# The head of a one-core SSM and FFN kernel: where the mean of the first two tiles is taken off, and how these tiles are loaded

## The chip, the core and the metric

The kernel runs on one NeuronCore of a Trainium2 chip. The metric is the device time of one execution in microseconds (us); the median of three runs is 178.27, from 178.15 to 178.41. The core has five engines with instruction streams of their own: TensorE (PE in the profile, its weight loads PEld), VectorE (DVE), ScalarE (ACT), GpSimd (POOL) and SyncE (SP), which here only issues transfers. Transfers (DMAs) are issued from the queues of SyncE, ScalarE and GpSimd and run beside the engines. SBUF is the on-chip memory, PSUM the memory that TensorE writes its results to, in eight banks.

## What is computed

The reference normalises x (2048 tokens of 512 features) over the features, feeds the result to a diagonal state-space layer A and to a gated feed-forward layer B, and adds both to x:

```
xn = (x - mean) / sqrt(var + 1e-5)
A:  Bu = xn @ B_bar.T;  h[t] = Lam_bar * h[t-1] + Bu[t];  y = 2 * Re(h @ C.T) + xn * Dskip
B:  (silu(xn @ w_gate) * (xn @ w_up)) @ w_down        # w_gate, w_up: 512 x 1376
out = x + A(xn) + B(xn)
```

Everything comes and goes in bfloat16. State and features are 512, so each is four blocks of 128.

## The kernel before

The 2048 tokens are 16 tiles of 128 rows, in four chunks of 512 tokens. TensorE multiplies along the partition axis, so the normalised tokens are wanted transposed, features on the partitions. For chunks 1 to 3 a transposing DMA does this. Chunk 0 can't wait for it. Its first three tiles go another way: they are transposed by TensorE, by a matmul against the identity matrix, and only their mean is taken off (`xcT`); the factor 1 / sqrt(var + eps) of a token (`rstd`) is applied later, as a per-row scale, when the product of tokens and weights leaves PSUM (`sw_gate`, `sw_up`).

The order of the work on every engine is the order in which the program writes it down; no scheduler moves it. Each engine runs its own list in that order and waits where an operand isn't ready.

The start of the program (lines 119 to 136) issues the loads. SyncE loads tile 0 of x, then four rows of the up weights (`wu01`, 256 KB each; a row is 128 of the 512 features), two rows of the gate weights (`wg01`), tile 2, a third gate row, tile 3, the fourth gate row, and more. ScalarE loads tile 1. A memset by VectorE (line 124) of two elements of tile 1 is written ahead of that load, so that it waits for it. From the third gate or x load of SyncE on, an issue waits for the landing of an earlier transfer, because the completion semaphores are used in turn.

The head proper begins at line 692. TensorE runs nine warm-up matmuls on constants (`dummy`, four of 512 columns and five of 128), into a bank that is not needed yet. VectorE makes `minus_mean`, the identity times -1/512, and sums each of the first two tiles over its features (`sum_dve`, line 221). Then, for tile i = 0 and 1 and feature block k:

- `raw_mm(i)` (line 233) transposes the four blocks of raw tile i into PSUM, one matmul of 128 columns each (line 230).
- `cT_mean(i, ...)` (line 237) adds the negative mean to one block or two, by a matmul of the broadcast sum with `minus_mean` that accumulates on the transposed block.
- `raw_copy(i, k)` (line 241) copies the block out of PSUM to `xcT` (a part of the tile CF in the profile), even blocks on ScalarE, odd ones on VectorE (line 245).

`row_mm` (line 712) then multiplies both tiles by one weight row at a time: for k = 0 to 3 four matmuls of 128x512 (two tiles, two groups of 512 columns) with the up weights, and after them the same with the gate weights. In the profile they are line 487. They use all eight PSUM banks. While the up rows run, VectorE takes the statistics of both tiles (line 182), and ScalarE takes the up products out with their scale (line 507). Tiles 2 and 3, the state-space scans on VectorE and the rest of the feed-forward layer follow; TensorE then works through all chunks.

Of the kernel before, what the change touches and what calls it, by code (L numbers as in the profile page):

```python
# [12 lines left out]
ALU = mybir.AluOpType  # L13
# [10 lines left out]
def kernel(  # L24
# [17 lines left out]
    nc = tc.nc  # L42
# [7 lines left out]
    NCH = L // CW  # L50
    TPC = CW // 128
    KD = D // 128
# [21 lines left out]
    def bank(shape=(128, CW), dtype=F32):  # L74
        return psum.tile(list(shape), dtype, name="ps")
# [4 lines left out]
    x_v = A_x[0].rearrange("(n p) d -> p n d", p=128)  # L80
# [5 lines left out]
    xall = const.tile([128, NT, D], BF16, name="xall")  # L86
    xnT = const.tile([128, NCH, KD, CW], BF16, name="xnT")
# [31 lines left out]
    HK = KD // 2  # L119
    ident = const.tile([128, 128], BF16, name="ident")  # L120
    make_identity(nc, ident[:])
    minus_mean = const.tile([128, 128], BF16, name="minus_mean")
    nc.sync.dma_start(out=xall[:, 0, :], in_=x_v[:, 0, :])
    nc.vector.memset(xall[:, 1, 0:2], 0.0)
    nc.scalar.dma_start(out=xall[:, 1, :], in_=x_v[:, 1, :])
    nc.scalar.preload_act_table_set("silu_and_others")
    for k in range(KD):
        load_row(nc.sync, wu01, wu_v, k)
# [49 lines left out]
    def by_k(ap):  # L178
        return ap.rearrange("p (k d) -> p k d", d=128)
# [30 lines left out]
    xcT, xc = CF[:, 0], CF[:, 1]  # L210
# [5 lines left out]
    sums = const.tile([128, 2], BF16, name="sums")  # L216
# [4 lines left out]
    def sum_dve(i, dst):  # L221
        nc.vector.scalar_tensor_tensor(out=xnT[:, NCH - 1, i, 0:HW], in0=xall[:, i, 0:HW], scalar=1.0,
                                       in1=xall[:, i, HW:D], op0=ALU.mult, op1=ALU.add, accum_out=dst)

    pair = [[[bank() for _ in range(2)] for _ in range(2)] for _ in range(2)]
    warm = pair[0][0][1]
    raw = [pair[0][1] + pair[1][0], pair[1][1] * 2]

    def cT_mm(ps, src, k, first, stop):
        nc.tensor.matmul(ps[:, k * 128:(k + 1) * 128], lhsT=src[:, k * 128:(k + 1) * 128], rhs=ident[:], start=first,  # L230
                         stop=stop)

    def raw_mm(i):
        for k in range(KD):
            cT_mm(raw[i][k], xall[:, i, :], k, all(p is not raw[i][k] for p in raw[i][:k]), False)

    def cT_mean(i, *ks):
        nc.tensor.matmul(by_k(raw[i][ks[0]][:])[:, ks[0]:ks[-1] + 1:HK], lhsT=sums[:, i:i + 1].to_broadcast([128, 128]),  # L238
                         rhs=minus_mean[:, None, :].to_broadcast([128, len(ks), 128]), start=False, stop=True)

    def raw_copy(i, k):
        cT_copy(V.tensor_copy if k % 2 else nc.scalar.copy, raw[i][k], i, k, k + 1)

    def cT_copy(copy, ps, i, k0=0, k1=KD):
        copy(out=xcT[:, k0:k1, i * 128:(i + 1) * 128], in_=by_k(ps[:, k0 * 128:k1 * 128]))
# [21 lines left out]
    V = nc.vector  # L267
# [398 lines left out]
    def dummy(ps, n, cols):  # L666
        for _ in range(n):
            nc.tensor.matmul(ps[:, 0:cols], lhsT=one.to_broadcast([128, 128]), rhs=one.to_broadcast([128, cols]),
                             start=True, stop=True)
# [20 lines left out]

    G, U = wg_g, wu_g
    dummy(warm, 4, CW)
    dummy(warm, 5, 128)
    nc.vector.tensor_scalar(out=minus_mean[:], in0=ident[:], scalar1=-1.0 / D, scalar2=None, op0=ALU.mult)
    for i in range(2):
        sum_dve(i, sums[:, i:i + 1])
    raw_mm(0)
    for k in range(HK):
        cT_mean(0, k)
        raw_copy(0, k)  # L700
    raw_mm(1)
    for k in range(HK, KD):
        cT_mean(0, k)
    for k in range(HK):
        cT_mean(1, k, k + HK)
        raw_copy(1, k)
    for k in range(HK, KD):
        raw_copy(0, k)
    for k in range(HK, KD):
        raw_copy(1, k)  # L710

    def row_mm(which, k):
        for i in range(2):
# [191 lines left out]
```

## Time and profile before

| | us |
|---|---|
| median of the runs | 178.27 (178.15 to 178.41) |
| span of the profiled execution | 175.8 |
| TensorE busy in the span | 171.4 (97%) |
| VectorE busy in the span | 156.9 (89%) |
| ScalarE busy in the span | 102.0 (58%) |
| first weight matmul (line 487) | starts at 4.98 |

The span runs from the first to the last instruction of the profiled execution. No time of its own outside the span is given for that execution; against the median of the runs 2.5 us lie around the span. In rows of a timeline the first number is the start in us from the span's beginning, the second the duration, then engine, line, operation, output and input, and how many instructions stand together; in brackets, how long the engine was idle before and what ended that. SPq and ACTq are issues of transfers. In rows of the transfers, the last number is the time from issue to landing in us. In grouped rows, the numbers behind the bar are the busy time in us, the mean of one in ns and the idle time before them. In rows by stretches of time, each engine has its busy time and a count, then come the granted TensorE clock, the busy share of the DMA engines and GB/s.

### The profile page before, as it was taken

How to read it: one execution, taken by the hardware profiler on the slowest of the kernel's cores; microseconds unless marked ns; L12 is line 12 of the kernel's file. 1: busy time of each engine (PE TensorE's matmuls, PEld its weight loads, DVE VectorE, ACT ScalarE, POOL GpSimd, SP SyncE). 2: the span in 40 equal slices, each digit the busy share in tenths (PEclk: the TensorE clock that was granted, in tenths of full speed). 3: DMA queues.
4: the chain of work that ended last, by engine and by line, in shares of the span. 5: the costliest groups of instructions: out<-in, count | busy, mean ns of one | idle time of the engine just before them, and what ended most of it. 6: DMA issues, size and time to landing. Idle time of an engine off the chain costs nothing.

```text
span 175.8 us, 2365 instructions
## 1 busy us (share of the span) xinstructions
PE 171.4 (97%) x847; PEld 82.6 (47%) x863; DVE 156.9 (89%) x259; ACT 102.0 (58%) x188; POOL 28.1 (16%) x39
## 2 busy tenths in 40 slices
PE   8999999999999999999999999999999999999993
PEld 4544446464444444446444444446444444444542
DVE  3776999999999999999999999999999998699542
ACT  3379498793997685236598660024666653990100
POOL 5244110032000000044300000025000000522500
PEclk9999999999999999999999999999999999999999
DMA  5998929999999300047016000007200000696921
GB/s 184 344 350 83 245 48 205 285 191 300 161 218 306 112 4 0 0 38 82 2 34 119 0 0 0 0 0 87 36 15 17 0 4 0 87 175 96 117 66 60
DMA packets 34043, 17.88 MB, mean 102 GB/s; under 512 B 24896, under 2 KB 32928, under 8 KB 33984
## 3 DMA queue, kind: packets, MB, share of 16 engines
q1 hardware_dynamic: 30288, 14.22, 34.1%
q0 software_dynamic: 3456, 3.28, 14.4%
q10 hardware_dynamic: 288, 0.23, 0.4%
q8 instruction: 7, 0.11, 0.3%
q14 instruction: 4, 0.03, 0.1%
HBM read 8.03 MB, written 5.24 MB: 75 GB/s over the span
## 4 chain that ended last, share of the span: by engine, by line
PE 96%; DMA 1%; issue 1%; DVE 0%
PE ps L455 29%; PE ps L598 22%; PE ps L611 16%; PE ps L380 16%; PE ps L487 8%; PE ps L541 3%; PE ps L771 2%; DMA xall<-in_A_x_dram 1%; PE ps L230 1%; PE ps L238 0%; DVE xall L614 0%; PE ps L271 0%
## 5 line engine op out<-in xcount | busy, mean ns | idle before, releaser
L598 PE MATMUL ps<-wd_sb,guT 128*128 128x512 bf16 (+4 forms) x184 | 38.7, 366 | 0.2
L422 DVE TENSOR_TENSOR_SCAN g<-r_t,car,u 128x512 bf16<-128x512 f32 x24 | 29.1, 1264 | 0.0
L611 PE MATMUL ps<-CF,wt 128*128 128x512 bf16 (+2 forms) x134 | 28.4, 366 | 0.1
L380 PE MATMUL ps<-xnT,BT 128*128 128x512 bf16 x125 | 28.1, 379 | 0.2
L598 PEld LDWEIGHTS <-guT 128*128 128x128 bf16 (+1 forms) x187 | 17.9, 98 | 20.5
L455 PE MATMUL ps<-xnT,wu 128*128 128x512 bf16 x95 | 24.6, 379 | 0.2
L455 PE MATMUL ps<-xnT,wg 128*128 128x512 bf16 x91 | 23.9, 379 | 0.1
L618 POOL DMA_DIRECT2D out_dram<-res x12 | 10.5, 1043 | 77.3 <-ACT res L617 72.1
L469 ACT ACTIVATE guT<-ps 128x512 bf16<-128x512 f32 x30 | 18.3, 609 | 4.8 <-PE ps L455 4.5
L470 ACT CAST u<-ps 128x512 bf16<-128x512 f32 x30 | 17.9, 596 | 4.6 <-PE ps L455 4.5
L382 ACT CAST u<-ps 128x512 bf16<-128x512 f32 x32 | 17.5, 597 | 4.8 <-PE ps L380 3.3
L611 PEld LDWEIGHTS <-wt 128*128 128x128 bf16 x136 | 13.0, 98 | 14.7
L380 PEld LDWEIGHTS <-BT 128*128 128x128 bf16 x128 | 12.5, 98 | 14.8
L617 ACT CAST res<-ps 128x512 bf16<-128x512 f32 x12 | 6.8, 583 | 21.0 <-PE ps L611 21.0
L572 ACT ACTIVATE xr<-xall,nb,rstd 128x512 bf16<-128x512 bf16 x16 | 11.8, 805 | 9.1 <-DVE xall L580 4.9
L455 PEld LDWEIGHTS <-wu 128*128 128x128 bf16 x96 | 9.4, 98 | 11.3
L455 PEld LDWEIGHTS <-wg 128*128 128x128 bf16 x96 | 9.3, 98 | 10.6
L192 POOL TENSOR_TENSOR rstd<-ve,neg_half 128x1 f32<-128x1 f32 (+1 forms) x7 | 7.6, 1079 | 29.4 <-DVE ve L191 29.0
L455 PE MATMUL ps<-xnT,w_end 128*128 128x512 bf16 x48 | 10.9, 379 | 0.0
L182 DVE BATCH_NORM_STATS2 stats<-xall 128x6 f32<-128x512 bf16 x16 | 10.8, 675 | 0.0
L474 DVE TENSOR_TENSOR guT<-guT,u 128x1024 bf16<-128x1024 bf16 x15 | 10.0, 675 | 0.0
L390 DVE TENSOR_TENSOR pm<-g,c 128x2048 bf16<-128x2048 bf16 x8 | 9.8, 1220 | 0.1
(120 smaller groups left out, 207.8 us busy)
## 6 DMA issues: line engine op xcount, KB each, us to landing
out_dram<-in_A_x_dram SPq DMA_DIRECT2D x3, 512.0 KB, 5.3
out_dram<-res POOLq DMA_DIRECT2D x12, 128.0 KB, 3.1
out_dram<-xall POOLq DMA_DIRECT2D x3, 512.0 KB, 6.0
wd_sb<-in_B_w_down_dram SPq DMA_DIRECT2D x1, 1280.0 KB, 8.2
wu<-in_B_w_up_dram SPq DMA_DIRECT2D x4, 256.0 KB, 3.8
wg<-in_B_w_gate_dram SPq DMA_DIRECT2D x4, 256.0 KB, 4.8
xall<-in_A_x_dram SPq DMA_DIRECT2D x1, 1024.0 KB, 7.0
xall<-in_A_x_dram SPq DMA_DIRECT2D x1, 512.0 KB, 6.1
```

What stands on the lines that cost most here:

```text
L182: nc.vector.bn_stats(out=stats[:, n, 0, :], in_=xall[:, n, :])
L380: nc.tensor.matmul(ps[:] if c else by_k(ps[:]), lhsT=BT[:, part, k, q * 128:(q + 1) * 128], rhs=xnT[:, c, k, :] if c else xnT0[:, k], star ...
L382: nc.scalar.copy(out=u_tiles[c][:, part, q, :], in_=ps[:])
L422: V.tensor_tensor_scan(out=g()[:, part, q, :], data0=r_t[:, q:q + 1].to_broadcast([128, CW]), data1=u_tiles[c][:, part, q, :], initial=ini ...
L455: nc.tensor.matmul(ps[:fs, lo:hi], lhsT=wslice(groups, fi, k), rhs=xnT[:, c, k, lo:hi], start=(k == 0), stop=(k == KD - 1))
L469: nc.scalar.activation(out=guT[:fs, fi, :], in_=psg[:fs], func=ACT.Silu)
L470: nc.scalar.copy(out=u_pair[c][:fs, fi % 2, :], in_=psu[:fs])
L487: nc.tensor.matmul(ps[:, 0:(b - a) * 128], lhsT=tokens(i, k), rhs=groups[gi][:, k, 0:(b - a) * 128], start=(k == 0), stop=(k == KD - 1))
L572: nc.scalar.activation(out=box["xr"][:], in_=xall[:, n, :], func=ACT.Identity, scale=rstd[:, n:n + 1], bias=nb[:, n:n + 1])
L598: nc.tensor.matmul(o[:], lhsT=gu_tiles[c][:fsz[fi], fi, i * 128:(i + 1) * 128], rhs=wd_sb[:fsz[fi], fi, lo:hi], start=(fi == 0), stop=False)
L611: nc.tensor.matmul(o[:], lhsT=w_tiles[c][:, part, q, i * 128:(i + 1) * 128], rhs=CF[:, part, q, lo:hi], start=False, stop=(part == 1 and q ...
L618: nc.gpsimd.dma_start(out=out_v[:, n, lo:hi], in_=res[:, lo:hi], accum_op=ALU.add)
```

## The change

Tiles 0 and 1 are each loaded in two pieces, rows 0 to 87 on SyncE's queue and rows 88 to 127 on ScalarE's; the memset is gone. The warm-up has three matmuls of 128 columns instead of five. The mean is no longer accumulated on the transposed blocks: `mean_mm` makes it once for a tile, 128 columns into a bank of its own (`low`). `raw_copy` takes two raw blocks at a time out of PSUM on ScalarE into SBUF (`xrT`, a part of `xnT` that is written much later), and `centered` on VectorE adds the negative mean from PSUM while writing `xcT`, first block by block for blocks 0 and 1 of both tiles, then blocks 2 and 3 together.

```diff
-    nc.sync.dma_start(out=xall[:, 0, :], in_=x_v[:, 0, :])
-    nc.vector.memset(xall[:, 1, 0:2], 0.0)
-    nc.scalar.dma_start(out=xall[:, 1, :], in_=x_v[:, 1, :])
+    XS = 88
+    for i in range(2):
+        nc.sync.dma_start(out=xall[0:XS, i, :], in_=x_v[0:XS, i, :])
+        nc.scalar.dma_start(out=xall[XS:128, i, :], in_=x_v[XS:128, i, :])
...
-    raw = [pair[0][1] + pair[1][0], pair[1][1] * 2]
+    raw, low = (pair[0][1], pair[1][0]), pair[1][1]
+    xrT = xnT[:, NCH - 2]
...
     def raw_mm(i):
         for k in range(KD):
-            cT_mm(raw[i][k], xall[:, i, :], k, all(p is not raw[i][k] for p in raw[i][:k]), False)
-
-    def cT_mean(i, *ks):
-        nc.tensor.matmul(by_k(raw[i][ks[0]][:])[:, ks[0]:ks[-1] + 1:HK], lhsT=sums[:, i:i + 1].to_broadcast([128, 128]),
-                         rhs=minus_mean[:, None, :].to_broadcast([128, len(ks), 128]), start=False, stop=True)
-
-    def raw_copy(i, k):
-        cT_copy(V.tensor_copy if k % 2 else nc.scalar.copy, raw[i][k], i, k, k + 1)
+            cT_mm(raw[i][k // HK], xall[:, i, :], k, k % HK == 0, k % HK == HK - 1)
+
+    def raw_copy(i, h):
+        k0, k1 = h * HK, (h + 1) * HK
+        nc.scalar.copy(out=xrT[:, k0:k1, i * 128:(i + 1) * 128], in_=by_k(raw[i][h][:, k0 * 128:k1 * 128]))
+
+    def mean_mm(i):
+        nc.tensor.matmul(low[i][:, 0:128], lhsT=sums[:, i:i + 1].to_broadcast([128, 128]), rhs=minus_mean[:],
+                         start=True, stop=True)
+
+    def centered(i, k0, k1):
+        at = slice(i * 128, (i + 1) * 128)
+        V.tensor_tensor(out=xcT[:, k0:k1, at], in0=xrT[:, k0:k1, at],
+                        in1=low[i][:, None, 0:128].to_broadcast([128, k1 - k0, 128]), op=ALU.add)
...
-    dummy(warm, 5, 128)
+    dummy(warm, 3, 128)
...
-    raw_mm(0)
-    for k in range(HK):
-        cT_mean(0, k)
-        raw_copy(0, k)
-    raw_mm(1)
-    for k in range(HK, KD):
-        cT_mean(0, k)
-    for k in range(HK):
-        cT_mean(1, k, k + HK)
-        raw_copy(1, k)
-    for k in range(HK, KD):
-        raw_copy(0, k)
-    for k in range(HK, KD):
-        raw_copy(1, k)
+    for i in range(2):
+        raw_mm(i)
+        mean_mm(i)
+        for h in range(2):
+            raw_copy(i, h)
+    for i in range(2):
+        for k in range(HK):
+            centered(i, k, k + 1)
+    for i in range(2):
+        centered(i, HK, KD)
```

## The prediction

> **What bounds the kernel now.** I read the page's engine shares first, then the chain that ended last, then the waits of TensorE, and only then the first ten microseconds as a timeline.
>
> ```profile
> span 175.8 us, 2365 instructions
> ...
> PE 171.4 (97%) x847; PEld 82.6 (47%) x863; DVE 156.9 (89%) x259; ACT 102.0 (58%) x188; POOL 28.1 (16%) x39
> ...
> PE 96%; DMA 1%; issue 1%; DVE 0%
> ```
>
> TensorE carries 96% of the chain; the only other visible piece, DMA 1%, is the first x tile. So anything that lets TensorE begin its weight matmuls earlier goes straight into the end, and nothing else does. The head shows when they begin. Columns are start, duration, engine, line, what it does.
>
> ```profile
> 0.74 0.39 SPq L123 DMA_DIRECT2D xall<-in_A_x_dram  x1
> ...
> 0.78 2.40 PE L668 MATMUL ps<-const-bfloat16-1.0 128*128 128x512 bf16 x9 [0.78 <-PEq L889]
> 0.81 0.06 DVE L124 MEMSET xall<- 128x1 uint32 x1 [0.81 <-PEq L889]
> ...
> 0.90 0.38 ACTq L125 DMA_DIRECT2D xall<-in_A_x_dram  x1
> ...
> 1.19 1.84 SPq L117 DMA_DIRECT2D wu<-in_B_w_up_dram  x4
> ...
> 1.31 1.28 ACT L126 ACT_TABLE_LOAD   x1 [1.31 <-DVE e_t L162]
> ...
> 3.24 0.42 DVE L222 SCALAR_TENSOR_TENSOR xnT<-xall 128x256 bf16<-128x256 bf16 x1 [1.70 <-DMA xall<-in_A_x_dram]
> ...
> 3.27 0.61 PE L230 MATMUL ps<-ident,xall 128*128 128x128 bf16 x4
> 3.59 0.08 DVE L222 DVE_READ_ACCUMULATOR xnT<-xall 128x1 bf16 x1
> ...
> 3.73 0.40 PE L238 MATMUL ps<-minus_mean,sums 128*128 128x128 bf16 x2
> ...
> 3.92 0.63 PE L230 MATMUL ps<-ident,xall 128*128 128x128 bf16 x4
> ...
> 4.35 0.79 PE L238 MATMUL ps<-minus_mean,sums 128*128 128x128 bf16 x4
> ...
> 4.98 3.62 PE L487 MATMUL ps<-wu,CF 128*128 128x512 bf16 x16
> 5.02 0.60 ACT L245 CAST CF<-ps 128x128 bf16<-128x128 f32 x3 [0.69 <-PE ps L238]
> ...
> 5.78 0.68 DVE L182 BATCH_NORM_STATS2 stats<-xall 128x6 f32<-128x512 bf16 x1
> ```
>
> Tile 0 is in at 3.24. From 3.27 to 4.98 TensorE does 14 small matmuls in order (8 transposes, 6 mean corrections), and only then the first weight matmul (L487). The 16 of these run without a gap: 3.62 less the last one's 0.38, over 15, is 0.216 us each.
>
> One thing decides what an earlier start is worth: the same shape costs different amounts before and after about 4.9 us.
>
> ```profile
> L668 PE MATMUL ps<-const-bfloat16-1.0 128*128 128x512 bf16 x4 | 1.9, 622 | 0.8 <-PEq L889 0.8
> ...
> L487 PE MATMUL ps<-wu,CF 128*128 128x512 bf16 x16 | 3.6, 379 | 0.0
> ```
> ```profile
> 0.00:1.00 1.00, 0.22 (x1) 0.14 (x2) 0.12 (x3) 0.00 (x0) 0.41 (x5) 1.00 0.00 0
> ```
>
> A 128x512 matmul takes 0.62 us from start to result among the warm-up matmuls and 0.38 among the weight matmuls, a difference of 0.24; so the pitch of a weight matmul would be about 0.216 + 0.22 = 0.43 in the early stretch. The six L238 of the timeline agree: the last four (768 columns) fill 4.35 to 4.98, 0.82 ns a column, against 0.42 later. The granted clock column reads 1.00 even in the first microsecond, so it does not show this; the durations do. TensorE therefore runs at half pace until about 4.95, and work begun before that gains only half of its head start.
>
> **The change, part by part.**
>
> *Loading.* One load on each queue becomes two on each, so SyncE issues one DMA more ahead of the weights. SyncE's pitch is 1.19 - 0.74 = 0.45, so all four wu rows, and the two wg rows behind them, are issued 0.45 later. From there on SyncE's later issues wait for earlier landings, as now. ScalarE no longer waits for VectorE's 0.06 us memset: it issues at about 0.75 instead of 0.90, and a second time at 1.2, which pushes its table load from 1.31 to about 1.65, with nothing for ScalarE to do before 3.4. Its cover is two microseconds.
>
> What x gains by this no row shows; these bound it. The first two are the landings (last column, us after issue) of tiles 0 and 1, then the four wu rows and the first wg row one by one, then 128 KB stores (L615) at the end, alone on the queues.
>
> ```profile
> xall<-in_A_x_dram SPq DMA_DIRECT2D x1, 128.0 KB, 2.5
> xall<-in_A_x_dram ACTq DMA_DIRECT2D x1, 128.0 KB, 2.6
> ...
> wu<-in_B_w_up_dram SPq DMA_DIRECT2D x1, 256.0 KB, 3.0
> ...
> wu<-in_B_w_up_dram SPq DMA_DIRECT2D x1, 256.0 KB, 3.6
> ...
> wu<-in_B_w_up_dram SPq DMA_DIRECT2D x1, 256.0 KB, 4.0
> ...
> wu<-in_B_w_up_dram SPq DMA_DIRECT2D x1, 256.0 KB, 4.4
> ...
> wg<-in_B_w_gate_dram SPq DMA_DIRECT2D x1, 256.0 KB, 4.7
> ...
> DMA to landing us min/median/max: 1.4/1.7/2.0
> ```
> ```profile
> 2.00:3.00 1.00, 1.00 (x7) 0.62 (x5) 0.00 (x0) 0.59 (x1) 1.00 (x2) 1.00 0.90 297
> ```
>
> Tile 0 (2.5 us) shares the engines with tile 1, issued 0.16 behind it; after the change all of tile 0 is issued first and tile 1 follows 0.45 behind. The best case is a transfer alone, 1.7 (a store, the nearest row without company): tile 0 in at 2.45. The worst is that the pieces balance badly and cost more: at 297 GB/s 128 KB take 0.44 us, and half of that on top gives 3.45. I take 2.2 us, midway between 1.7 and 2.5 because two thirds of the company goes: tile 0 at 2.94, and tile 1, issued at 1.2, at 3.40 (now 0.90 + 2.6 = 3.50).
>
> The wu rows are issued at a pitch of 0.47 but land at 4.19, 5.25, 6.1, 7.0, and wg's first at 7.77: 0.8 to 1.1 apart. They stand in a backlog, and a later issue is mostly absorbed. The bounds are 0 and 0.45 later; I take 0, since the gaps between landings are near twice the issue pitch. Needed are they at 4.98, 5.84, 6.71, 7.57 and 8.43 (four matmuls of 0.216 a row), so the slack is 0.8, then 0.59, 0.6, 0.57 and 0.66.
>
> *TensorE.* 14 small matmuls become 10: 8 transposes and one 128-column mean for each tile. Removed are 4 x 128 + 2 x 256 columns, plus 2 x 128 needed now, so 768 columns at 0.82 ns, 0.63 us of the stretch from 3.27 to 4.98. Two warm-up matmuls fewer end 0.21 us earlier, at about 2.76 instead of 2.97 (0.78 + 2.40, less the 0.2 by which a result follows its columns), ahead of the x tile: nothing by itself.
>
> *ScalarE and VectorE.* Four copies each of 128x128 on both become four of 128x256 on ScalarE and, on VectorE, four additions of 128x128 and two of 128x256 that read PSUM. Durations:
>
> ```profile
> L245 ACT CAST CF<-ps x5: 267/271/586, 4.1 to 11.5; 128x128 bf16<-128x128 f32 x4, 128x512 bf16<-128x512 f32 x1
> L245 DVE CAST CF<-ps x4: 280/286/293, 4.2 to 5.6; 128x128 bf16<-128x128 f32 x4
> ```
> ```profile
> 172.10 0.56 DVE L614 TENSOR_TENSOR xall<-ps,xall 128x384 bf16<-128x384 f32 x1 [0.61 <-PE ps L611]
> 173.17 0.29 DVE L614 TENSOR_TENSOR xall<-ps,xall 128x128 bf16<-128x128 f32 x1 [0.51 <-PE ps L611]
> ```
>
> ScalarE: 0.27 for 128 columns, 0.59 for 512, so 0.37 for 256; three in 0.60 means that the next begins 0.10 before the end, pitch 0.27. VectorE's addition with one operand in PSUM: 0.29 for 128 columns, 0.56 for 384, so 0.42 for 256; pitch 0.2 and 0.34.
>
> *The new chain*, with 0.04 for each handover:
> - sums: tile 0 from 2.96, out at 3.39; tile 1 from 3.42, out at 3.85.
> - TensorE: tile 0's transposes from 2.97, pitch 0.107, result 0.31 after start; its mean from 3.45, out 3.76; tile 1's from 3.56.
> - ScalarE: tile 0's halves 3.43 to 3.80 and 3.70 to 4.07, tile 1's 4.02 to 4.39 and 4.29 to 4.66.
> - VectorE: first block of tile 0 from 3.87 to 4.16, the second to 4.36, the first of tile 1 4.43 to 4.72, the second to 4.99, the wide ones to 5.32 and 5.66.
>
> The first weight matmul starts at 4.20; its wu row is in at 4.19. It takes 0.43 to 4.63; the second has 0.32 / 0.43 of its columns done by 4.95 and ends at 5.00. The third, on tile 1, is ready since 4.72 + 0.04 and starts at 5.00. It starts now at 4.98 + 2 x 0.216 = 5.41. **Sum: 0.41 us earlier.** The next rows are then wanted at 5.43, 6.30, 7.16 and 8.02 and land at 5.25, 6.1, 7.0 and 7.77: ahead by 0.16 to 0.25. VectorE's statistics start after 5.6, now 5.78; they stay off the path.
>
> What would be late next far behind the head: the coefficients CF for the first output tile.
>
> ```profile
> 67.18 5.38 DVE L366 SCALAR_TENSOR_TENSOR CF<-CT,nc2im,cm 128x512 bf16<-128x512 bf16 x8
> ...
> 72.67 2.54 PE L611 MATMUL ps<-CF,wt 128*128 128x512 bf16 x11
> ```
>
> The last of the eight is ready at 72.56 and used by the eighth matmul, 72.67 + 7 x 0.216 = 74.2, so 1.6 us of slack covers 0.41 even if VectorE does not move at all.
>
> The span of 175.8 and 2.5 us around it make the median of 178.27; 175.8 - 0.41 + 2.5 gives 177.9.
>
> A page of the notes speaks against the split: the Trainium skill, "DMA: Bandwidth & Descriptors", section "Why a DMA increments its semaphore by 16 and not by 1", says that a load runs on the largest number of engines up to 16 that divides its row count, and on the lowest-numbered ones. By it 88 rows go to 11 engines and 40 to 10, so ten engines carry 12 rows of a tile instead of 8. No row of the profile separates engines; its sum would be that of the first rival below.
>
> **The rivals.**
> 1. *The weights come too late.* Uneven pieces, or the later issue, hold the weight rows back. At the 0.44 us that a tile takes, half as much again on the busiest engines is 0.2 a tile, 0.4 for both; the later issue is 0.45. Of a slack of 0.57 there remain 0.12 to 0.17, so 178.1. For it: the just-in-time landings above. Against: the backlog. Slower than now only from a delay over 0.57.
> 2. *The half-pace stretch lasts longer* (the other side). It ends now 4.1 us after the first warm-up matmul at 0.78. If fewer warm-up matmuls and the new gap before the first weight matmul (4.10, behind tile 1's mean, to 4.20) make it start over at 4.2, it ends at 8.3, and the work from 4.95 to 8.3 loses 3.35 / 2 = 1.7: 178.27 + 1.7 - 0.41 = 179.6. It decides from a release at 5.8 (twice 0.41 past 4.95). Against: TensorE idles 0.30 before tile 0 now too (2.97 to 3.27). The Trainium skill, "TensorE: Matmul & The Clock Gate", Part 1, describes such a gate, half rate until a window of about 3.4 us has been busy; the doubling near 4.9 agrees with it, the granted clock column does not show it.
> 3. *The two-step copy is slower than costed.* ScalarE and VectorE in series have replaced both in parallel; tile 1's first block would have to be 0.7 late (5.4 instead of 4.72) to lose. At an addition of 0.69, VectorE's price for 512 columns, for each of three blocks it is 0.6 late: 178.2.
>
> **How the numbers follow.** A measurement of this kernel tells about 0.2%, 0.36 us, from no change. My forecast case (by itself 177.7 to 178.0: with tile 0 at 2.45 the wu row at 4.19 still sets the start, and with tile 0 at 3.24 the first block is 0.3 later, so that half of it, 0.15, is lost) has 0.60: 0.44 of it faster, 0.16 within. Rival 1 has 0.19: 0.14 within, 0.05 slower. Rival 2 has 0.13, slower. Rival 3 has 0.08: 0.06 within, 0.02 slower. Together faster 0.44, same 0.36, slower 0.20. The range of 177.6 to 178.6 takes in rivals 1 and 3 and a release of the half pace up to 6.4 (0.32 lost), and leaves out the rest of rival 2; its low end is 0.1 under the forecast's own.
>
> **What would show it.** Right: the first sum on VectorE before 3.1, the first weight matmul near 4.2, 16 of them without a gap, and every later stage 0.3 to 0.4 earlier. Wrong: the first sum at 3.3 or later (split), weight matmuls waiting for wu or wg (rival 1), weight matmuls at 0.43 after 5 us (rival 2), TensorE waiting for VectorE's additions past 5.1 (rival 3).

## The result: 2.36 us slower

The changed kernel takes 180.53 us in the median of six runs (180.13 to 181.44), the kernel before 178.17 in six runs beside it (177.88 to 178.41). The ratio is 1.0134, 95% interval 1.0115 to 1.0154: slower by 2.36 us. The forecast was 177.9, so the time moved the other way, and it lies far outside the range of 177.6 to 178.6.

The profile's page of the changed kernel, in the order in which that of the kernel before was read:

```profile
span 179.3 us, 2379 instructions
...
PE 174.4 (97%) x857; PEld 82.6 (46%) x857; DVE 157.7 (88%) x260; ACT 104.2 (58%) x188; POOL 28.3 (16%) x39
...
PE 95%; DMA 1%; DVE 1%; ACTq 0%; issue 0%; DVEq 0%
```

TensorE still carries the chain, and is busy 3.0 us longer than before (174.4 against 171.4), although the program gives it six matmuls fewer (863 weight loads before, 857 now). A part of the 3.0 is not real, since the trace of before has only 847 of its 863 matmuls. On the chain VectorE now has 1% (before 0%), and a piece of ScalarE's transfer queue (ACTq) is new; both belong to the head, so that is where to look. Its timeline, columns as before:

```profile
0.74 0.92 ACTq L126 DMA_DIRECT2D xall<-in_A_x_dram  x2
0.74 0.79 SPq L125 DMA_DIRECT2D xall<-in_A_x_dram  x2
...
0.78 2.19 PE L676 MATMUL ps<-const-bfloat16-1.0 128*128 128x512 bf16 x7 [0.78 <-PEq L893]
...
1.57 1.78 SPq L117 DMA_DIRECT2D wu<-in_B_w_up_dram  x4
...
3.30 0.42 DVE L223 SCALAR_TENSOR_TENSOR xnT<-xall 128x256 bf16<-128x256 bf16 x1 [1.76 <-DMA xall<-in_A_x_dram]
3.33 0.59 PE L232 MATMUL ps<-ident,xall 128*128 128x128 bf16 x4 [0.36 <-DMA xall<-in_A_x_dram]
...
3.99 0.42 DVE L223 SCALAR_TENSOR_TENSOR xnT<-xall 128x256 bf16<-128x256 bf16 x1 [0.26 <-DMA xall<-in_A_x_dram]
4.01 0.61 PE L232 MATMUL ps<-ident,xall 128*128 128x128 bf16 x4
...
4.48 0.29 PE L244 MATMUL ps<-minus_mean,sums 128*128 128x128 bf16 x1
5.41 6.26 PE L495 MATMUL ps<-wu,CF 128*128 128x512 bf16 x16 [0.64 <-DVE CF L249]
```

and, from the view of the transfers, the landing of the first weight row (last column, us after its issue at 1.57):

```profile
wu<-in_B_w_up_dram SPq DMA_DIRECT2D x1, 256.0 KB, 3.8
```

Tile 0 is no earlier (first sum at 3.30, before 3.24), tile 1 is later (3.99). The small matmuls end at 4.77, and then TensorE is idle for 0.64 us. The view puts that wait to VectorE, but the first centred block is loaded as a weight at 4.67; what comes in at 1.57 + 3.8 = 5.37 is the first up row. Before it came in at 4.19.

What follows the gap is worse than the gap: 16 weight matmuls take 6.26 us, where they took 3.62. The weight matmuls one stretch after another (us, of the 128x512 shape alone; the mean in ns is the figure ahead of the last bar), at 9 to 9.5, 10.5 to 11, and 11.5 to 12:

```profile
L495 PE MATMUL ps<-wu,CF 128*128 128x512 bf16 x2 | 1.1, 634 | 0.0
...
L495 PE MATMUL ps<-wu,CF 128*128 128x512 bf16 x3 | 1.2, 517 | 0.0
...
L495 PE MATMUL ps<-wg,CF 128*128 128x512 bf16 x3 | 0.8, 379 | 0.0
```

634 ns is the price at half pace, 379 at full pace: the half pace, over at 4.95 in the profile of before, lasts here until about 11. The chain that ended last puts a price on it. Of the kernel before, and then of the changed one (start, length, what): the first 20 weight matmuls, the first of chunk 0's projection, the last addition.

```profile
5.14 4.32 PE ps L487 x20
...
22.69 6.91 PE ps L380 x32
...
173.17 0.29 DVE xall L614
```
```profile
5.41 7.12 PE ps L495 x20
...
25.76 6.91 PE ps L388 x32
...
176.24 0.29 DVE xall L622
```

The start costs 0.27, the 20 matmuls 7.12 - 4.32 = 2.80. At twice the pitch half of a stretch is lost, so 2.80 is 5.6 us of half pace from 5.41, to 11.0, as the durations say. The 3.07 are there at the projection and still there, to a hundredth, at the last addition: nothing gives any of it back. The spans to two decimals are 179.29 and 175.85, a difference of 3.44. So another 3.44 - 3.07 = 0.37 us lies behind the last addition.

These two executions stand at opposite ends of their kernels' runs: 179.3 is the longest span of the changed kernel (178.0 to 179.3), 175.8 nearly the shortest of the one before (175.7 to 176.8, median 176.2, in the 25 runs beside the first experiments). By the medians the difference is 2.36 us, and the experiments have to divide these.

### The profile page after: what moved, and what is told of

The parts are those of the page before. It is cut to its first block, busy times and chain, and to the rows that moved or that the text cites. A ratio compares the mean times of both kernels' runs of the same rounds, so it can differ in the third digit from the quotient of the medians.

```text
span 179.3 us, 2379 instructions
## 1 busy us (share of the span) xinstructions
PE 174.4 (97%) x857; PEld 82.6 (46%) x857; DVE 157.7 (88%) x260; ACT 104.2 (58%) x188; POOL 28.3 (16%) x39
## 3 DMA queue, kind: packets, MB, share of 16 engines
HBM read 8.03 MB, written 5.24 MB: 74 GB/s over the span
## 4 chain that ended last, share of the span: by engine, by line
PE 95%; DMA 1%; DVE 1%; ACTq 0%; issue 0%; DVEq 0%
PE ps L463 29%; PE ps L606 21%; PE ps L619 15%; PE ps L388 15%; PE ps L495 9%; PE ps L549 3%; PE ps L775 2%; DMA xall<-in_A_x_dram 1%; DVE CF L249 0%; ACTq L126 0%; DVE xall L622 0%; DVE xnT L223 0%; PE ps L232 0%; PE ps L279 0%; DVEq L249 0%
## 5 line engine op out<-in xcount | busy, mean ns | idle before, releaser
L463 PE MATMUL ps<-xnT,wg 128*128 128x512 bf16 x96 | 24.6, 379 | 0.0
L626 POOL DMA_DIRECT2D out_dram<-res x12 | 10.5, 1042 | 80.1 <-ACT res L625 74.5
```

Source lines behind the costliest of these rows:

```text
L463: nc.tensor.matmul(ps[:fs, lo:hi], lhsT=wslice(groups, fi, k), rhs=xnT[:, c, k, lo:hi], start=(k == 0), stop=(k == KD - 1))
L626: nc.gpsimd.dma_start(out=out_v[:, n, lo:hi], in_=res[:, lo:hi], accum_op=ALU.add)
```

## The experiments

The theory at the start: the late up row opens a gap in TensorE, and the gap prolongs the half pace. The rival: one of the two parts is slow by itself. So first each part alone, the gap filled, and a gap without the parts.

**The loads alone.** The kernel before with the changed load block:

```diff
-    nc.sync.dma_start(out=xall[:, 0, :], in_=x_v[:, 0, :])
-    nc.vector.memset(xall[:, 1, 0:2], 0.0)
-    nc.scalar.dma_start(out=xall[:, 1, :], in_=x_v[:, 1, :])
+    XS = 88
+    for i in range(2):
+        nc.sync.dma_start(out=xall[0:XS, i, :], in_=x_v[0:XS, i, :])
+        nc.scalar.dma_start(out=xall[XS:128, i, :], in_=x_v[XS:128, i, :])
```

> The kernel before with the split loads alone (88 rows on SyncE's and 40 on ScalarE's queue, no memset); mean path and warm-up of before. Theory A (the split loads delay the first up row to about 5.4 us, TensorE idles, and its half pace lasts past 5 us): first weight matmul at 5.2 to 5.5, half pace for some of the weight matmuls, 179.0 to 180.7 us. Rival B (the two-step mean path through ScalarE and VectorE is the cause): 178.2 us, as before. Rival C (both are needed): between, about 178.6.

Measured: 179.18 us (178.81 to 181.05; 178.25 for the kernel before), ratio 1.0064, 1.0035 to 1.0093. The first up row and the chain:

```profile
wu<-in_B_w_up_dram SPq DMA_DIRECT2D x1, 256.0 KB, 3.7
```
```profile
4.65 0.64 PE ps L239 x4
...
5.31 4.62 PE ps L488 x20
```

The row is nearly as late as in the changed kernel (1.57 + 3.7 = 5.27), but the 14 small matmuls last until 5.29, so hardly any gap opens, and the 20 matmuls lose 0.30 instead of 2.80. Cutting the loads costs 0.93 us by itself; that not all of this lies in the head comes out at the end.

**The mean path alone.** The changed kernel with the load block of before (whole tiles).

> The changed kernel with the loads of before (tile 0 whole on SyncE, memset, tile 1 whole on ScalarE); two-step mean path and three short warm-up matmuls stay. Theory A: x tiles at 3.24 and 3.5, first up row at 4.2, first weight matmul at about 4.5, half pace until about 5, 177.9 to 178.3 us. Rival B (mean path is the cause): 179.5 us or more, with TensorE waiting for VectorE.

Measured: 178.30 (177.87 to 178.54; before 178.25), ratio 0.9993, 0.9976 to 1.0010.

```profile
4.29 0.31 PE L243 MATMUL ps<-minus_mean,sums 128*128 128x128 bf16 x1
4.53 4.39 PE L494 MATMUL ps<-wu,CF 128*128 128x512 bf16 x16
```

The first weight matmul starts 0.45 us earlier, as the prediction's sum has it once its 4.20 is moved by the 0.3 us that tile 0 is later here. No gain is seen: 16 matmuls take 4.39 instead of 3.62, since the half pace goes on to about 6.2 in this execution. At half pace the 0.45 could be worth no more than 0.22, and the interval, 0.43 faster to 0.18 slower, does not exclude that. So neither part alone makes 2.36: 0.93 + 0.05 is 1.0.

**The gap filled.** The changed kernel with work on constants behind the two transposed tiles:

```diff
     for i in range(2):
         raw_mm(i)
         mean_mm(i)
         for h in range(2):
             raw_copy(i, h)
+    dummy(warm, 8, 128)
```

> The changed kernel with eight more matmuls of 128 columns on constants between tile 1's mean and the first weight matmul, about 0.85 us that fill the idle time from 4.6 to 5.4. Theory A (the idle time lengthens the half pace): first weight matmul still at about 5.4, but full pace from 5 to 7.5 us instead of 10.8, 178.6 to 179.4 us. Rival D (the late up row costs by itself, the idle time does not matter to the pace): unchanged, 180.5 us.

Measured: 179.59 (178.94 to 179.89; before 178.25), ratio 1.0072, 1.0052 to 1.0092: 0.94 us less than the changed kernel (1.02, if each is compared with the kernel before that ran beside it), for eight matmuls whose result nobody reads. No run of one kernel reaches into the range of the other.

```profile
4.43 0.77 PE L676 MATMUL ps<-const-bfloat16-1.0 128*128 128x128 bf16 x8
5.04 1.02 PE L495 MATMUL ps<-wu,CF 128*128 128x512 bf16 x4
6.76 2.82 PE L495 MATMUL ps<-wu,CF 128*128 128x512 bf16 x12 [0.70 <-DMA wu<-in_B_w_up_dram]
```

The weight matmuls now run at full pace from the first (four in 1.02). In this execution the half pace was over at about 4.7, before the gap of the changed kernel would have begun, so it is the medians that show what the filling does. The row shows something else: the second up row comes in at 6.72, TensorE idles 0.70 for it, and the twelve matmuls behind that run at full pace (2.82). In this execution a gap that comes once the full pace is reached costs itself and no more.

**A gap without the parts.** The kernel before with only two long warm-up matmuls, no transfer touched:

```diff
-    dummy(warm, 4, CW)
...
-    dummy(warm, 5, 128)
+    dummy(warm, 2, CW)
```

> The kernel before with only two warm-up matmuls of 512 columns instead of four and five short ones; TensorE idles from about 1.65 to 3.27, no transfer is touched. Theory A (an unbroken stretch of about 4.1 us ends the half pace): half pace until about 7.4 us, (7.4 - 4.95) / 2 = 1.2 us lost, 178.9 to 179.9 us. Rival D (idle time before the real work does not matter): 178.2 us.

Measured: 179.44 (178.84 to 179.75), ratio 1.0064, 1.0044 to 1.0083.

```profile
3.08 0.61 PE L230 MATMUL ps<-ident,xall 128*128 128x128 bf16 x4 [1.29 <-DMA xall<-in_A_x_dram]
...
4.80 5.34 PE L487 MATMUL ps<-wu,CF 128*128 128x512 bf16 x16
```

Idling alone, at a time when TensorE had nothing to do anyway, costs 1.2 us: the weight matmuls start earlier than before (4.80), but 16 take 5.34, and the half pace ends at about 8.3. That is the mechanism by itself.

**Why the row is late.** Four suspects: the later issue of the weights, the simultaneous start of two queues, the uneven cut, or cutting at all. First an even cut, alone and with the mean path (`XS = 64` in place of 88), and whole tiles with both on SyncE, so that the weights are issued as late as in the changed kernel:

```diff
-    nc.sync.dma_start(out=xall[:, 0, :], in_=x_v[:, 0, :])
-    nc.vector.memset(xall[:, 1, 0:2], 0.0)
-    nc.scalar.dma_start(out=xall[:, 1, :], in_=x_v[:, 1, :])
+    for i in range(2):
+        nc.sync.dma_start(out=xall[:, i, :], in_=x_v[:, i, :])
```

> As the kernel with the split loads alone, but cut at row 64, so that both pieces of a tile have 64 rows; queues, order and number of transfers unchanged. Theory E (88 and 40 rows divide badly over the 16 DMA engines, so that a few carry more): first up row back at 4.2 to 4.7 instead of 5.3, 178.2 to 178.6 us. Rival F (one transfer more ahead of the weights on SyncE) and rival G (both queues start at once and hinder each other): first up row still at 5.1 or later, 179.2 us.

> The changed kernel with the cut at row 64 instead of 88. Theory E, with the half pace that idle time lengthens: the idle time ahead of the first weight matmul shrinks with the earlier up row, 178.2 to 178.8 us. Rivals F and G: as the changed kernel, 180.5 us.

> The kernel before with both tiles loaded whole by SyncE, one after the other, and nothing by ScalarE (no memset). Weights are issued about 0.45 us later, as with the split loads, but every transfer has 128 rows and one queue starts alone. Rival F: first up row at 5 or later, 179.2 us. Theories E and G: first up row at 4.2 to 4.7, 178.2 to 178.5 us.

Measured: the even cut alone 179.82 (ratio 1.0079, 1.0059 to 1.0099), with the mean path 180.44 (1.0106, 1.0067 to 1.0146), both whole tiles on SyncE 178.37 (1.0001, 0.9988 to 1.0015). Of the even cut, and then of the two whole tiles:

```profile
L125 SPq DMA_DIRECT2D xall<-in_A_x_dram x2: 573/699/825, 0.7 to 1.4; - x2
```
```profile
wu<-in_B_w_up_dram SPq DMA_DIRECT2D x1, 256.0 KB, 2.7
```

Even pieces don't help. Here the row takes only 3.0 us from its issue, but that is pushed to 2.24, because SyncE's issues of x take 0.57 and 0.83 us (0.39 in the kernel before); it lands at 5.24 all the same. With whole tiles the row is issued at 1.65, even later than in the changed kernel, and lands at 4.3. So the later issue alone does not make the row 1.2 us late. It may still cost something: in two kernels further down with the same loads the row is issued at 1.65 too and lands at 4.6 and 4.8.

**Simultaneous whole tiles, one queue for all pieces, and a cut at 96.** The kernel before without the memset of line 124 (both tiles start together); the cut loads with all four pieces on SyncE; and `XS = 96`.

> The kernel before without the memset on tile 1, so that ScalarE's load of tile 1 starts together with SyncE's load of tile 0; both whole tiles, one transfer on each queue. Theory G (two queues that issue at the same moment hinder each other): SyncE's first issue takes longer than 0.39 us or its tile lands later than 3.3, first up row at 4.4 or later, 178.4 to 178.9 us. Rival H (it takes the split into four pieces): as before, 178.3 us, tile 0 at 3.1 to 3.25.

> The kernel with the split loads alone, but all four pieces (88, 40, 88, 40 rows) on SyncE's queue, mean path of before. The weights are issued later, about 2.1 us, so the time from their issue to landing is what counts. Rival E' (88 and 40 rows occupy only some of the 16 DMA engines): first up row 3.5 us or more after its issue, as with two queues (3.7 to 3.8). Rival G' (two queues whose pieces are in flight at once hinder each other): 2.5 to 3.0 us after its issue, each piece of x in 2.2 us or less.

> The kernel with the split loads alone, cut at row 96, so that pieces have 96 and 32 rows, both multiples of 16, on two queues. Rival E': first up row 2.5 to 3.0 us after its issue, and in at 4.3 to 4.6 if the issues take 0.4 us as with 88 and 40. Rival I (pieces that go to all 16 engines stretch the issues, as with 64 and 64, 0.55 to 0.83 us each): first up row issued at 2.0 us or later and in at about 5. Rival G': 3.5 us or more after its issue.

Measured: 178.45 (ratio 1.0006, 0.9989 to 1.0023), 179.60 (1.0083, 1.0045 to 1.0121) and 179.43 (1.0074, 1.0041 to 1.0108). The first up row of the three, in that order:

```profile
wu<-in_B_w_up_dram SPq DMA_DIRECT2D x1, 256.0 KB, 3.1
```
```profile
wu<-in_B_w_up_dram SPq DMA_DIRECT2D x1, 256.0 KB, 3.4
```
```profile
wu<-in_B_w_up_dram SPq DMA_DIRECT2D x1, 256.0 KB, 3.2
```

Starting together costs the weights next to nothing (1.19 + 3.1 = 4.3). The pieces of 88 and 40 rows slow the row on one queue too (3.4, against 2.7 behind whole tiles on the same queue), and there it is issued at 2.32, lands at 5.7 and is waited for. At 96 rows it lands at 4.9. So in these profiles every way of cutting into four makes the first up row late, by the transfer or by the issue. One profile a kernel is little, however: with pieces of 88 and 40 rows on two queues the row took 3.8, 3.7, 3.6, 3.4 and 2.8 us in the five kernels that have them, and behind whole tiles 2.7 to 3.1 in nine kernels; 96 rows with 3.2 are hardly outside that. The Trainium skill, "DMA: Bandwidth & Descriptors", section "Why a DMA increments its semaphore by 16 and not by 1", would have it that 88 and 40 rows use 11 and 10 engines and 96 and 32 use all 16. The packets of ScalarE's queue in the first 7 us (the first number of the row) agree with the 10 and the 16. They are, for the kernel before (one whole tile), the changed one (two pieces of 40 rows) and that with 96 (two of 32):

```profile
q10 hardware_dynamic: 144, 0.13, 5.4%
```
```profile
q10 hardware_dynamic: 100, 0.08, 5.3%
```
```profile
q10 hardware_dynamic: 96, 0.07, 2.9%
```

A row of x is 1 KB and one packet; what is left over is 16 for the whole tile, 10 for each piece of 40 rows and 16 for each of 32, as many as the engines. The 3.7 against 3.2 agrees with the rule in direction, too. It is not the whole of it: the kernel with 96 rows is still 1.26 us slower than the one before. About 0.4 of this lies at the end of the program (below); for the remaining 0.8 its profile shows no wait.

**Can the earlier start be kept?** The mean path on whole tiles with three more short warm-up matmuls; with both tiles on SyncE; and this with three short matmuls ahead of the weight matmuls as well.

> Loads of before, two-step mean path, and six short warm-up matmuls instead of three, so that TensorE's idle time ahead of tile 0 shrinks from 0.3 to about 0.03 us. Theory A (idle time lengthens the half pace): 0.1 to 0.4 us less than with three, 177.9 to 178.2 us. If so small a gap does not matter: 178.3 us.

> Both tiles whole on SyncE's queue, two-step mean path, three short warm-up matmuls. Tile 0 at 2.8, tile 1 at 3.3, first up row at 4.3. If the mean path gains 0.4 us once x and the weights are in time: first weight matmul at 4.35, 177.8 to 178.1 us. If the end of the half pace decides and takes the gain: 178.3 us.

> As the kernel with both tiles on SyncE and the two-step mean path, with three more short matmuls on constants ahead of the first weight matmul, 0.32 us, to fill the time until the first up row is in. Theory A: half pace ends no later than without them on average, 0 to 0.3 us less than that kernel. Otherwise equal.

Measured: 178.26 (ratio 0.9999, 0.9978 to 1.0019), 178.79 (1.0041, 1.0018 to 1.0064) and 178.86 (1.0041, 1.0014 to 1.0069). The first starts its weight matmuls at 4.33 and is no faster. The other two spread from 178.31 to 180.57 and from 177.89 to 180.32, where the kernel before keeps within 177.85 and 178.84 over 28 runs: these two heads are sometimes as quick as before and sometimes 2 us slower, and filling 0.3 us ahead of the weights did not mend that. No version here beats the kernel before.

**Where the half pace ends, over all profiles.** The durations of the matmuls show it in each of the 18 profiles. In 15 of them TensorE, once it has begun at 0.78, waits at most about 0.4 us at a stretch while it is at half pace. There the end lies anywhere from about 4.1 to 7.2, which is 3.4 to 6.4 us behind the beginning. The weight matmuls of both whole tiles on SyncE, where TensorE does not wait at all, and of all pieces on one queue:

```profile
4.68 4.64 PE L486 MATMUL ps<-wu,CF 128*128 128x512 bf16 x16
```
```profile
5.80 4.16 PE L488 MATMUL ps<-wu,CF 128*128 128x512 bf16 x16 [0.36 <-DMA wu<-in_B_w_up_dram]
```

At full pace 16 take 3.62, so the half pace ends at about 4.68 + 2 x 1.02 = 6.7 and 5.80 + 2 x 0.54 = 6.9. In the three other profiles TensorE waits longer at half pace: in the changed kernel 0.64, in the kernel before with two warm-up matmuls 1.29, and in the changed kernel with the even cut 0.59. There the end lies 4.7 to 5.6 us behind the end of that wait. The even cut, with 5.26 + 2 x 2.36 = 10.0:

```profile
5.26 5.98 PE L495 MATMUL ps<-wu,CF 128*128 128x512 bf16 x16 [0.59 <-DVE CF L249]
```

One reading fits all 18. The half pace ends between 3.4 and 6.4 us after TensorE has begun to work, at a moment that differs from execution to execution; a wait of about 0.6 us at half pace starts that time anew, one of 0.4 does not. By it, idling until 3.08 instead of working from 0.78 moves the end by 2.3 us on average and costs half of that, 1.15 (an estimate); measured were 1.2. It makes the 4.95 of the kernel before an early end, and the spread of that kernel from one run to the next (spans of 175.7 to 176.8, 1.1 us) is no larger than ends 3 us apart can give, 1.5. The reading was made from these profiles afterwards, and no run was made to test it.

**The end of the program.** All kernels with cut loads, and none of the others so far, have the extra 0.37 us behind the last addition, and their waits of SyncE differ at the program's last line. Kernel before, then the changed one (total us, times, longest):

```profile
SPq L900 <- DMA out_dram<-xall: 0.5, 1, 0.5
```
```profile
SPq L904 <- DMA out_dram<-xall: 1.0, 2, 0.5
```

The records of the trace behind these rows show a list: SyncE waits for the counters of the transfers in a fixed order, 0.06 us each if they are done. The transfers that SyncE and ScalarE issue (40 before, 42 after) use eight of these in turn. Start in us and counter, before on the left; the last store uses counter 109 and lands at 174.92, after it uses 103 and lands at 178.01:

```
before                     after
173.93  102                177.44  100   (next-to-last store)
...                        178.03  103   (last store)
174.24  107                178.09  104
174.36  108                ...
174.94  109 (last store)   178.33  108
                           178.39  109
```

Before, the last store is the last in the list, and the checks of all others pass while it travels. With two transfers more it stands second of eight, and six checks come behind its landing, 6 x 0.06 = 0.36. If that is so, the number of transfers decides and not how x is loaded. So: the kernel before with the three copies of x to the output at 52 us issued as five (42 transfers, head untouched), and the cut loads, alone and with the mean path, with those three issued as one (40 again):

```diff
-    for a in range(0, (NCH - 1) * CW, CW):
-        nc.sync.dma_start(out=out[0, a:a + CW, :], in_=A_x[0, a:a + CW, :])
+    nc.sync.dma_start(out=out[0, 0:3 * CW, :], in_=A_x[0, 0:3 * CW, :])
```

> The kernel before with the three copies of x to the output at 52 us (line 856) issued as five, so SyncE and ScalarE issue 42 transfers in all, as in the changed kernel, and the head is untouched. Theory: the eight completion semaphores are used in turn, so the last store then uses one that SyncE's last line waits for early, and the rest of that list of waits comes behind its landing: two waits for stores at the last line instead of one, and about 0.4 us more at the end, 178.7 against 178.3. Rival: the 0.4 us at the end belongs to the cut loads themselves; then this kernel stays at 178.3 with one wait.

> The kernel of the first experiment (both tiles in pieces of 88 and 40 rows, the rest as before) with the three copies of x to the output at 52 us issued as one, so the number of transfers is that of the kernel before. Theory: one wait for a store at the last line, and 0.4 us less than the first experiment's 179.18: about 178.75, the rest being the head. Rival: two waits and 179.2.

> The changed kernel with the three copies of x to the output at 52 us issued as one. Theory: 0.4 us less than 180.53, about 180.1; what is left over the kernel before, about 1.9 us, is the head alone. Rival: 180.5.

Measured: 178.75 (178.13 to 179.02; before 178.18), ratio 1.0029, 1.0019 to 1.0039; 178.71, ratio 1.0035, 1.0022 to 1.0048; 180.08, ratio 1.0104, 1.0090 to 1.0118. The same row of the three:

```profile
SPq L900 <- DMA out_dram<-xall: 1.0, 2, 0.5
```
```profile
SPq L900 <- DMA out_dram<-xall: 0.5, 1, 0.5
```
```profile
SPq L903 <- DMA out_dram<-xall: 0.5, 1, 0.5
```

Two transfers more cost the kernel before 0.57, two less give 0.47 back to the cut loads and 0.45 to the whole change. The 0.37 of the list lies within the interval of the first (0.34 to 0.70). The term is the turn of the counters and has nothing to do with the head.

The profiled execution of the last one shows by chance the changed head without its late row, which came in at 1.57 + 2.8 = 4.37:

```profile
wu<-in_B_w_up_dram SPq DMA_DIRECT2D x1, 256.0 KB, 2.8
```
```profile
4.66 5.25 PE ps L495 x20
```

No gap ahead of the weight matmuls, and 20 of them in 5.25 instead of 7.12. This execution is no pattern for the median: its span is 176.3, that of the three others 177.7 to 178.0; and its time of 179.8 has 3.5 us around the span instead of their 2.3, which stays unexplained.

## Why the prediction was wrong

By the medians the 2.36 us divide so: 0.45 at the end of the program (the last experiment); 0.53 from the cut loads in the head (178.71 - 178.18); 0.05 from the mean path alone, which can't be told from nothing; and the rest, 2.36 - 1.03 = 1.3, only where both parts meet. Filling the gap took 0.94 of these 1.3 away.

- **"The bounds are 0 and 0.45 later; I take 0": the step that failed first.** The first row is 1.18 us later (5.37 against 4.19). Of this, 0.38 is the later issue and 0.80 the transfer, which took 3.8 us instead of 3.0 from issue to landing. The backlog argument looked at the issue alone (both whole tiles on SyncE, issued 0.46 later: in at 4.3 in one profile, at 4.6 and 4.8 in two others, so not always absorbed). The bound was too tight: the sentence on the divided rows, priced at "0.2 a tile, 0.4 for both", was kept to the first rival and not to the bound. There it was set against the slack one at a time with the later issue, 0.4 or 0.45; both came, and added up to twice the slack of 0.57.
- **"tile 0 at 2.94, and tile 1, issued at 1.2, at 3.40": wrong.** 3.30 and 3.99 by the sums. The price of a store alone at the end of the program does not carry over to a cut load at its start; even two whole tiles one after the other, on one queue, took 2.1 us each. (The 2.2 that was taken is also not midway between 1.7 and 2.5, which is 2.1.) With tile 0 at 3.24 the text gave away only 0.15, so this alone would have mattered little.
- **"TensorE therefore runs at half pace until about 4.95", held fixed in the sum: the dear error.** The end of the half pace depends on what TensorE does before it, and 4.95 was an early one besides. The second rival said the first of these, had the side and the size of the loss right (1.7; where both parts meet it is 1.3 by the medians, and 2.80 in the profile), and got 0.13. It looked for the trigger in a gap of 0.10, and had against it that 0.30 of idling do not start the half pace over; the profiles bear that out up to about 0.4. The trigger was the first rival, the late row, which was priced by the start alone and "Slower than now only from a delay over 0.57". The two were treated as alternatives; in fact the first sets off the second. The delay of the start is worth 0.27 in the profile, the gap that it opens 2.80. The shorter work for TensorE, the point of the change, is what leaves room for the gap: with 14 small matmuls the same late row cost 0.53 in the head.
- **"0.63 us of the stretch": mis-sized, and nothing is seen of it.** With whole loads the stretch from the first transpose to the first weight matmul is 1.22 us instead of 1.71, 0.49 shorter, and that matmul starts at 4.53, 0.45 earlier than before. In the time no gain can be told from nothing.
- **ScalarE and VectorE: right.** Predicted 0.37 for the copy and 0.29 and 0.42 for the additions; measured, in the changed kernel:

```profile
L241 ACT CAST xnT<-ps 128x256 bf16<-128x256 f32 x4 | 1.3, 375 | 0.8 <-PE ps L232 0.8
...
L249 DVE TENSOR_TENSOR CF<-xnT,ps 128x128 bf16<-128x128 bf16 x4 | 1.0, 282 | 0.1
L249 DVE TENSOR_TENSOR CF<-xnT,ps 128x256 bf16<-128x256 bf16 x2 | 0.7, 414 | 0.0
```

  The third rival did not come up.
- **"The span of 175.8 and 2.5 us around it": mis-sized.** In the runs 2.0 us lie around the span of the kernel before; the profiled execution was one of its quickest, about 0.4 under the median span. So the 4.95, too, was that of a quick execution.
- **Left out altogether: the end of the program.** "From there on SyncE's later issues wait for earlier landings, as now" followed the completion counters through the head, and not to the last line, where their turn is worth about 0.45.
- **That the head goes "straight into the end": right**, with the other sign: 3.07 at the projection, 3.07 at the last addition.

What stays open: why the half pace ends where it does when TensorE hardly waits, anywhere within 3 us. With the cut at 96 rows no wait is seen and the weight matmuls still take 634 ns until past 6; the kernel before without its memset does the same in its profile, with an unchanged median. For 0.8 us of what the cut at 96 rows costs no cause is shown. And that the row behind pieces of 88 and 40 rows is slower is seen in four profiles of five, but its reason only in part.

## What to carry to other kernels

Before work ahead of a dense stretch of matmuls is shortened, ask what TensorE does with the time: if it waits for a transfer while it is still at half pace, the wait is paid again in the pace of what follows, here with 2.80 us for a gap of 0.64; eight matmuls on constants were worth 0.94 us here, while a wait of 0.70 at full pace cost only itself. Read the end of the half pace from several profiles, since a single one shows only one of many ends (4.1 to 7.2 here). The small loads at the start were better whole in this kernel: all four ways of cutting them that were tried cost time, 0.93 to 1.44 us by themselves, of which some 0.4 lie at the end of the program. And a change in the number of transfers has a price at the last line of the program, which the waits of SyncE show: count it in, and see that the last store is the last that is waited for.

## What was not expected of the hardware

- A gap of 0.64 us in TensorE, or an idle 1.3 us much earlier, put the end of the half pace at about 11 and 8.3 us, that is 5.6 us behind the end of the gap in the one and 5.2 in the other, while the column of the granted clock reads 1.00 in the head of both the changed kernel and the one before. The Trainium skill, "TensorE: Matmul & The Clock Gate", Part 1, has a window of about 3.4 us that must be busy, and says that it runs freely and does not start with the kernel. A stretch that begins inside one window would have to fill the next, which puts the end 3.4 to 6.8 us behind its beginning (an estimate from that page's figure); the 3.4 to 6.4 of the profiles agree with it.
- The same 256 KB load took 2.7, 3.0, 3.4 or 3.8 us from issue to landing in profiles that differ in how the 256 KB of x ahead of it were cut and queued, and 2.8 in another execution with the cut that had 3.8.
- The two issues of 64-row pieces on SyncE took 0.57 and 0.83 us, 1.5 and 2.1 times what a whole tile takes (0.39).
